# A fused attention pair: the weight stream in twelve slices through four places, and another order of the first loads

## The chip, the cores and the metric

The kernel runs on one core of one Trainium2 chip. What counts is the device time of one execution in microseconds (us). Before the change three runs took 1550.25, 1554.49 and 1554.56 us, so the median is 1554.49 us.

## What is computed

Two attentions read the same x (1 x 2048 x 640, bf16) and are mixed by a gate.

```python
g = sigmoid((x * gate_w).sum(-1, keepdims=True))
a = A(x)          # 64 segments in turn, each needs the memory of the one before
b = B(x)          # local, dilated
out = g * a + (1 - g) * b

# A: H = 32 heads of 192, segment of 32 tokens, 8 memory rows
for s in range(64):
    h = concat([mem, x[32*s : 32*s+32]])             # 40 rows of 640
    q, k, v = h @ Wq, h @ Wk, h @ Wv                 # each W is 640 x 6144
    p = softmax(mask(q @ k.T * 192**-0.5))           # per head
    o = (p @ v) @ Wo                                 # Wo is 6144 x 640
    mem = o[:8];  outs.append(o[8:])

# B: 32 heads of 20; each position looks at 8 positions, 2 apart, backwards
q, k, v = split(x @ wqkv);  b = (softmax(q . k[pos - 2*j]) @ v) @ wo
```

A's weights are four matrices of 640 x 6144 bf16, 31 MB in all. They don't all fit into the core's on-chip memory beside the working tiles, and each of the 64 segments needs all of them.

## The kernel before

**Stages.** Part B comes first (0 to about 187 us). Behind it a prepass (to about 345 us) works out what of A's q, k and v doesn't depend on the running memory. Then part A runs: segment 0 on its own, 62 segments in a loop (380 to 1461 us), the last segment, and `part_z`, which makes the rows of the output that the memory rows stood for.

**Slices of A's weights.** A's weights are cut into slices: `("q", p, kc)` and `("k", p, kc)` with 15 of each, `("v", t, kc)` with 15, `("oa", i)` with 12 and `("ob", i)` with 8. A slice of q, k or v has 128 rows of 2048 bf16 numbers (4096 bytes a row, 512 KB), one of oa or ob 128 rows of 1536 (384 KB). A fourth or third index in the key (`_is_half`) makes it a half slice: 256 KB or 192 KB. `_parts` says whether a slice is used whole or as two halves.

**Resident and streamed.** Most slices stay in the core for all of part A. `weights_setup` (L511) orders them and deals them out: the first `N_EARLY` are loaded in part B, the next `N_EARLY2` and then `late` follow as memory of other stages becomes free, and the last `N_LAST` in segment 0 (`load_late(2)`, L1045). The tiles of the late ones are named `wlate_...`. What is in the list `STREAM` is loaded again in every segment, through `SLOTS` places (tiles `wst0`, `wst1`, ...), in the order in which TensorE uses it. `pump` (L558) issues the next load on SP's queue whenever the place that it falls to is free; the place of load n is n modulo `SLOTS`. `release` (L566) marks a place free when TensorE has issued the last matmul that reads its slice, and calls `pump`. The load itself waits on SP, at L562, until those matmuls have ended. So each place is in one of three states: in use, being filled, or waiting filled. Before the change 21 half slices go through seven places of 2 KB a partition.

**Order.** In part A, and in part B from `order.enter_context` on (L400), the order of instructions on each engine is the one written. Ahead of that point, for the short block's projection `proj(0, n, c)` (L379 to L381), the order comes from a scheduler. The loop's segments are cut into stages (`stage`, L788): at each boundary every engine, SP too, waits for what the stage before left open (L1133 is the line that these waits carry). In the loop no loads are issued between `held()` and the next `stage()`.

**Part B's beginning.** Part B works in blocks of 484 positions and one short block ahead of them (block 0). `proj(b, n, c)` (L263) makes 128 rows of q or k of a block and stores them to DRAM on SP's queue (L276); `load_qk` (L278) reads them back with the heads laid out afresh, as `bqT` and `bkT`, four loads for each; `scores` (L296) needs these. `load_xT(b, ...)` (L190) loads 512 tokens of x. `make_v` (L252) makes v; `gates` (L225) the gate. `bulk` (L390) is a list of loads that are issued a few at a time by `fetch`: x, B's output weights, the early resident slices, and for the prepass the columns of Wq.

**The prepass** reads Wq and Wk by columns (`get_columns`, L588), from resident slices where there are any, and otherwise by loads into the places of the stream, which aren't used for streaming yet: on SP's queue for q, on POOL's for k. The slices of v that aren't resident are loaded there on POOL's queue (`get_slice`).

Of the kernel before, what the change touches and what calls it, by code (L numbers as in the profile page):

```python
# [10 lines left out]
BF = mybir.dt.bfloat16  # L11
F32 = mybir.dt.float32
I32 = mybir.dt.int32

SLOTS = 7
N_EARLY = 15
N_EARLY2 = 12
N_LAST = 7
LATE0 = 71680
STREAM = [("q", 0, 1, 1), ("k", 0, 1, 1), ("k", 0, 3, 1), ("q", 1, 1, 0), ("k", 1, 0, 0), ("k", 1, 3, 1), ("q", 2, 2,  # L20
          0), ("k", 2, 0, 1), ("k", 2, 1, 1), ("k", 2, 4, 1), ("v", 0, 3, 1), ("v", 1, 1, 0), ("v", 1, 4, 1), ("v", 2,
          0, 1), ("v", 2, 3, 0), ("oa", 3, 1), ("oa", 4, 1), ("ob", 2, 0), ("oa", 7, 0), ("oa", 11, 0), ("ob", 6, 0)]

STEP_PE = 3.4

# [7 lines left out]
def _width(key):  # L33
    n = 1536 if key[0] in ("oa", "ob") else 2048
    return n // 2 if _is_half(key) else n

def _parts(key):
    halves = [key + (h,) for h in range(2)]
    return halves if any(k in STREAM for k in halves) else [key]

# [53 lines left out]
class _K:  # L94
# [59 lines left out]
    def part_b(self, outer):  # L154
# [11 lines left out]
        with ExitStack() as ctx:  # L166
# [23 lines left out]
            def load_xT(b, q, t0=0, t1=512):  # L190
                return q.dma_start(xT[:, :, HALO + 512 * b + t0:HALO + 512 * b + t1], self.laid["xT"][:, :, 512 * b + t0:512 * b + t1])
# [5 lines left out]
            load_xT(0, nc.sync)  # L197
            nc.scalar.dma_start(gw[:], self.laid["gw"].unsqueeze(2))
            nc.scalar.dma_start(wv[:], self.laid["wv"])
            load_xT(1, nc.sync)  # L200
            ones = wp.tile([128, 32], BF, name="b_ones")
            nc.vector.memset(ones[:], 1.0)
            band = wp.tile([128, NQ], BF, name="band")
# [71 lines left out]
                self.evac(t[:, 0:nn], ps[:, 0:nn], "dve" if n == 0 or b > 1 else "act")  # L275
                nc.sync.dma_start(qk_dram[b, n][128 * c:128 * c + 128], t[:, 0:nn])  # L276

            def load_qk(b, queue=None):  # L278
                for n in range(2):
                    nn = shape_of(b)[0] * shape_of(b)[1] + n * HALO  # L280
                    for hh in range(4):
                        (queue or nc.sync).dma_start(QK[n][b % 2][32 * hh:32 * hh + 20, :, 0:nn], heads(qk_dram[b, n], 0, 8, hh))
# [93 lines left out]
            nc.scalar.preload_act_table_set("natural_log_exp_and_others")  # L376
            assert S % 512 == 0 and nb == 5
            steps = [(b, g) for b in range(nb) for g in range(8)]
            for c in range(KC):  # L379
                for n in range(2):  # L380
                    proj(0, n, c)  # L381
# [12 lines left out]
            def fetch(n):  # L394
                for f, *a in bulk[:n]:
                    f(*a)
                del bulk[:n]

            order = ExitStack()
            order.enter_context(tc.manual_schedule(engines={mybir.EngineType.PE, mybir.EngineType.Activation, mybir.EngineType.DVE,  # L400
                                                            mybir.EngineType.SP, mybir.EngineType.Pool}))
            fetch(1)
            make_v(0, range(2))
            proj(1, 0, 0)
            proj(1, 1, 0)
            load_qk(0, nc.scalar)
            gates(0)

            def fill(what):
                for w in what:  # L410
# [24 lines left out]
            rest = tasks  # L435
# [57 lines left out]
    def v_columns(self, t, kc):  # L493

        out = []
        for k in _parts(("v", t, kc)):
            sl = self.get_slice(k)
            out += [sl[:, f:f + 512] for f in range(0, _width(k), 512)]
        return out
# [11 lines left out]
    def weights_setup(self):  # L511
        nc, tc = self.nc, self.tc
        rest = [k for u in _slice_keys() for k in _parts(u) if k not in STREAM]
        first = ["q", "k", "v", "oa", "ob"]
        rest = sorted(rest, key=lambda k: first.index(k[0]))
        self.early, self.early2, late = rest[:N_EARLY], rest[N_EARLY:N_EARLY + N_EARLY2], rest[N_EARLY + N_EARLY2:]
        self.late = ([], [], late[-N_LAST:])
        used = 0
        for k in late[:-N_LAST]:
            used += 2 * _width(k)  # L520
            self.late[int(used > LATE0)].append(k)
        self.wres = self.ctx.enter_context(tc.tile_pool(name="wres", bufs=1))
        self.res_tiles = {}
        at = _places()[0]
        self.packed = {k: self.laid["slices"][n:n + 128 * _width(k)].rearrange("(p f) -> p f", p=128) for k, n in at.items()}
        self.wscr = self.packed
        self.wstream = self.ctx.enter_context(tc.tile_pool(name="wstream", bufs=1))
        self.slots = [self.wstream.tile([128, 1024], BF, name=f"wst{i}") for i in range(SLOTS)]
        self.slot_at, self.streaming, self.pending = 0, False, []

    def load(self, key, t):
# [42 lines left out]
    def get_slice(self, key):  # L574
        if key in self.res_tiles:
            return self.res_tiles[key]
        n = _width(key)
        if self.streaming:
            assert STREAM[self.used] == key and self.used < self.sent
            t = self.slots[self.used % SLOTS][:, 0:n]  # L580
            self.used += 1
            return self.view(t, key)
        t = self.slots[self.slot_at % SLOTS][:, 0:n]
        self.slot_at += 1
        self.nc.gpsimd.dma_start(t, self.wscr[key])
        return self.view(t, key)

    def get_columns(self, m, h):  # L588

        W = {"q": self.Wq, "k": self.Wk}[m].rearrange("(c p) f -> p c f", p=128)  # L590
        p, x = h // 2, h % 2
        out = {}
        for kc in range(self.KC):
            if (m, p, kc) in self.res_tiles:
                t = self.res_tiles[m, p, kc][:, 1024 * x:1024 * x + 1024]
            else:
                t = self.slots[self.slot_at % SLOTS]
                self.slot_at += 1
                (self.nc.sync if m == "q" else self.nc.gpsimd).dma_start(t[:], W[:, kc, 1024 * h:1024 * h + 1024])
            out[kc] = [t[:, f:f + 128] for f in range(0, 1024, 128)]  # L600
        return out

# [97 lines left out]
    def part_a(self):  # L700
# [4 lines left out]
        with ctx:  # L705
# [28 lines left out]
                        return x[:, f:f + 32]  # L734

            st = [Px[2], Px[1], KW[:, 512:1024], Px[2]]
            st4 = self.slots[1][:, 768:1024], Px[0][:, 0:256]
            st5 = (P[1][:, 1:5, 0:8, :].rearrange("p b c i -> p b (c i)"), Px[0][:, 256:512])

            psm = ctx.enter_context(tc.tile_pool(name="psm", bufs=1, space=bass.MemoryType.PSUM))  # L740
# [44 lines left out]
            def segment(part, prev, s, nxt, looped=False):  # L785
# [278 lines left out]
                if nxt is None:  # L1064
                    self.oz, self.oz_keys = {}, {}
                    self.oz_free = [k for p in range(3) for m in "qk" for k in self.res_tiles if k[:2] == (m, p) and len(k) == 3]
                    self.oz_free += [k for k in self.res_tiles if k[0] == "v" and len(k) == 3]
                    self.b4_free = [k for k in self.res_tiles if k[0] in "vqk" and len(k) == 4]
                    self.load_oz(0)
                if nxt is not None:  # L1070
                    load_seg(nxt)
# [97 lines left out]
    def part_z(self, psm, wo, tail):  # L1169

        nc = self.nc
        oz = self.oz
        kept = self.kept.values()
        for i, k in enumerate(k for k in STREAM if k in wo and k not in kept):
            t = self.res_tiles[self.b4_free[4 + i]][:, 0:_width(k)]
            nc.sync.dma_start(t, self.wscr[k])
            wo[k] = self.view(t, k)
        for n in range(1, 4):
            if n > 1:
                self.load_oz(n)  # L1180
            self.sort_oz(n)
        for n in range(4):
            b4 = self.res_tiles[self.b4_free[n]][:, 0:640]
            rows = lambda ap: ap.rearrange("(n s t) f -> n s t f", n=4, t=32)[n, :, 24:32, :]
            nc.scalar.dma_start(b4.bitcast(I32).rearrange("p (j f) -> p j f", j=4),
                                self.bsc_dram.rearrange("(n s t) j f -> n s t j f", n=4, t=32)[n, :, 24:32, :, 0:80])
            for part, f0, nf in (("oa", 0, 384), ("ob", 384, 256)):
                ps = psm[int(part == "ob")]
                for c in range(48):
                    R, j, t = c // 12, c // 3 % 4, c % 3  # L1190
                    for q in range(4):
                        nc.tensor.matmul(ps[32 * q:32 * q + 32, 0:nf],  # L1192
                                         lhsT=oz[n, q][:, 24 * (1 - R // 2) + 6 * j + 3 * (R % 2) + t, :],
                                         rhs=self.o_weights(wo, part, c), start=(c == 0), stop=(c == 47),
                                         tile_position=(0, 32 * q), skip_group_check=True)
                nc.vector.scalar_tensor_tensor(out=b4[:, f0:f0 + nf], in0=ps[:, 0:nf], scalar=self.gZ[:, n:n + 1],  # L1196
                                               in1=b4[:, f0:f0 + nf], op0=ALU.mult, op1=ALU.add)
            nc.sync.dma_start(rows(self.out2d), b4)
            if n == 0:
                tail()  # L1200
# [63 lines left out]
```

## Time and profile before

| what | value |
|---|---|
| median of the runs | 1554.49 us |
| the profiled execution | 1550.84 us |
| its span (first to last instruction) | 1548.8 us |
| part B, prepass | 0 to about 187, to about 345 us |
| segment 0 | 345.6 to about 376 us |
| the loop, 62 iterations | 379.7 to 1461.2 us, 17.445 us each |
| last segment and `part_z` | to 1548.8 us |
| TensorE busy (matmul, by the profile's model) | 1459.2 us, 94% |
| bytes moved | 446.3 MB, mean 288 GB/s |

PE is TensorE, PEld its weight loads, DVE VectorE, ACT ScalarE, POOL GpSimd, SP the engine that only issues DMAs; "SPq" is SP's queue. A row such as `L916 PE MATMUL psm<-wst,aHa` is the matmuls of line 916 that read a place of the stream (`wst`) and a working tile (`aHa`) and write into the tile `psm`. The clock in the profile is the TensorE clock that was granted, where 1.00 is full speed. The DMA share is the mean busy share of the core's 16 DMA engines. In the list of DMA issues, the last number is the median time from issue to landing. All times are of one profiled execution.

### The profile page before, as it was taken

How to read it: one execution, taken by the hardware profiler on the slowest of the kernel's cores; microseconds unless marked ns; L12 is line 12 of the kernel's file. 1: busy time of each engine (PE TensorE's matmuls, PEld its weight loads, DVE VectorE, ACT ScalarE, POOL GpSimd, SP SyncE). 2: the span in 40 equal slices, each digit the busy share in tenths (PEclk: the TensorE clock that was granted, in tenths of full speed). 3: DMA queues.
4: the chain of work that ended last, by engine and by line, in shares of the span. 5: the costliest groups of instructions: out<-in, count | busy, mean ns of one | idle time of the engine just before them, and what ended most of it. 6: DMA issues, size and time to landing. Idle time of an engine off the chain costs nothing. (4 is left out here: it accounts for less than half of the span.)

```text
span 1548.8 us, 91126 instructions
## 1 busy us (share of the span) xinstructions
PE 1459.2 (94%) x36746; PEld 821.3 (53%) x36746; DVE 815.6 (53%) x2256; ACT 642.7 (41%) x1673; POOL 205.9 (13%) x432
## 2 busy tenths in 40 slices
PE   5988899997999999999999999999999999999978
PEld 3444444443555555555555555555555555555557
DVE  1787533333555555555555555555555555555510
ACT  1587532222443444344443444444444444344430
POOL 0000200200111111111111111111111111111100
PEclk9999999998999999999999999999999999999989
DMA  6778896788999999999999999999999999999970
GB/s 174 199 194 229 275 310 167 178 264 284 303 318 321 333 322 316 316 329 322 325 323 330 327 326 317 321 337 324 327 322 326 324 324 321 328 322 329 314 192 16
DMA packets 365435, 446.30 MB, mean 288 GB/s; under 512 B 123864, under 2 KB 227848, under 8 KB 365368
## 3 DMA queue, kind: packets, MB, share of 16 engines
q1 hardware_dynamic: 271080, 395.47, 77.7%
q10 hardware_dynamic: 80736, 25.44, 6.9%
q0 software_dynamic: 13552, 24.47, 4.9%
q8 instruction: 46, 0.75, 0.2%
q14 instruction: 21, 0.17, 0.0%
HBM read 407.04 MB, written 38.20 MB: 287 GB/s over the span
## 5 line engine op out<-in xcount | busy, mean ns | idle before, releaser
L825 ACT CAST aP<-psx 128x512 bf16<-128x512 f32 x128 | 68.7, 589 | 358.2 <-PE psx L818 358.2
L980 PEld LDWEIGHTS <-aP 128*32 128x32 bf16 x6144 | 162.7, 96 | 63.9 <-ACT aP L959 20.3
L916 PE MATMUL psm<-wlate_v,aHa 128*32 128x512 bf16 x2048 | 189.6, 381 | 1.1 <-issue 1.1
L818 PEld LDWEIGHTS <-aHa 128*32 128x32 bf16 x4608 | 120.1, 96 | 119.1 <-issue 20.6
L980 PE MATMUL psm<-wlate_oa,aP 128*32 128x384 bf16 x2560 | 167.7, 329 | 0.0
L840 DVE STREAM_TRANSPOSE aK<-aP 128x512 bf16<-128x512 bf16 (+1 forms) x256 | 135.0, 546 | 7.6 <-ACT aP L825 0.8
L980 PE MATMUL psm<-wst,aP 128*32 128x384 bf16 (+1 forms) x896 | 121.4, 306 | 7.4 <-DMA wst<-in_slices_dram 7.4
L980 PE MATMUL psm<-wlate_ob,aP 128*32 128x256 bf16 x2688 | 125.8, 274 | 1.0 <-issue 1.0
L818 PE MATMUL psm<-wres_q,aHa 128*32 128x512 bf16 x1280 | 119.2, 382 | 7.4 <-PEq L1133 5.2
L959 DVE CAST aP<-psx 128x128 bf16<-128x128 f32 (+2 forms) x192 | 75.6, 422 | 80.2 <-PE psx L947 80.1
L837 DVE STREAM_TRANSPOSE aP<-aP 128x512 bf16<-128x512 bf16 (+1 forms) x128 | 74.1, 579 | 79.1 <-ACT aP L825 79.1
L916 PE MATMUL psm<-wlate_v,aHb 128*32 128x512 bf16 x1152 | 115.2, 379 | 0.0
L818 PEld LDWEIGHTS <-aHb 128*32 128x32 bf16 x3072 | 77.3, 96 | 60.5 <-issue 3.0
L818 PE MATMUL psx<-wres_k,aHa 128*32 128x512 bf16 x896 | 108.1, 381 | 0.0
L925 ACT CAST aP<-psm 128x256 bf16<-128x256 f32 (+1 forms) x192 | 85.9, 447 | 47.7 <-PE psS L870 46.3
L959 ACT CAST aP<-psS 128x384 bf16<-128x384 f32 (+2 forms) x192 | 65.3, 374 | 72.5 <-PE psx L947 48.3
L756 POOL DMA_DIRECT2D aVz<-zv_dram x64 | 34.3, 535 | 443.2 <-DMA wst<-in_slices_dram 397.1
L818 PE MATMUL psx<-wst,aHa 128*32 128x512 bf16 x512 | 88.5, 382 | 2.1 <-DMA wst<-in_slices_dram 2.1
L818 PE MATMUL psm<-wres_q,aHb 128*32 128x512 bf16 x1024 | 80.4, 381 | 0.0
L916 PEld LDWEIGHTS <-aHa 128*32 128x32 bf16 x2304 | 54.7, 97 | 46.4 <-issue 16.4
L749 POOL DMA_DIRECT2D aK<-in_xh_dram x63 | 34.4, 546 | 329.0 <-PE psm L916 289.1
L941 PEld LDWEIGHTS <-aP 32*128 32x128 bf16 (+1 forms) x4096 | 43.4, 97 | 64.5 <-DVE aK L907 32.8
(181 smaller groups left out, 3222.3 us busy)
## 6 DMA issues: line engine op xcount, KB each, us to landing
wst<-in_slices_dram SPq DMA_DIRECT2D x960, 256.0 KB, 4.7
wst<-in_slices_dram SPq DMA_DIRECT2D x384, 192.0 KB, 3.8
zpk_dram<-ZS ACTq DMA_DIRECT2D x6, 2048.0 KB
aP<-zpk_dram SPq DMA_DIRECT2D x64, 192.0 KB, 3.9
wres_q<-in_slices_dram SPq DMA_DIRECT2D x12, 512.0 KB
aVz<-zv_dram POOLq DMA_DIRECT2D x64, 96.0 KB, 4.4
wlate_v<-in_slices_dram SPq DMA_DIRECT2D x10, 512.0 KB
wst<-in_A_Wk_dram POOLq DMA_DIRECT2D x14, 256.0 KB, 5.9
```

The source lines that it names most:

```text
L749: nc.gpsimd.dma_start(xh, row(self.xh_dram, s))
L756: nc.gpsimd.dma_start(vz[:], self.zv_dram[bass.ds(8 * s, 8)].rearrange("i r f -> r i f"))
L818: burst([nc.tensor.matmul(pq[32 * j:32 * j + 32, :], lhsT=hT[kc], rhs=sl[j], start=(kc == 0), stop=(kc == KC - 1), tile_position=(0, 32 * ...
L825: nc.scalar.copy(st[i], pqs[i])
L837: nc.vector.transpose(P[p][:, 1:5, c0:c1, :].rearrange("p b c i -> p c b i"), x)
L840: nc.vector.transpose(KT[:, c0:c1, :].rearrange("p c k -> p (c k)"), x)
L916: burst([nc.tensor.matmul(pvs[t][32 * j:32 * j + 32, :], lhsT=hT[kc], rhs=sl[j], start=(kc == 0), stop=(kc == KC - 1), tile_position=(0, 3 ...
L925: (nc.vector.tensor_copy if t == 0 else nc.scalar.copy)(Px[t][:, cs], pvs[t][:, cs])
L941: ms.append(nc.tensor.matmul(out[:, r, t, :], lhsT=v_block(2 * h + r, t)[ks, f0 - 128 * t:f1 - 128 * t], rhs=E[ks, par, EA.start + 40 * r: ...
L959: (nc.scalar.copy, nc.vector.tensor_copy)[g](x.rearrange("p (j c q) -> p j c q", j=2, q=32), pairs[g][:, :, 0:240].rearrange("p j (c q) -> ...
L980: ms.append(nc.tensor.matmul(pso[part][32 * jj:32 * jj + 32, 0:n], lhsT=oT_slot(R // 2, j, 3 * (R % 2) + t), rhs=self.o_weights(osl, part, ...
```

## The change

**The stream.** `STREAM` names twelve slices in place of 21 halves: six whole slices of q, k and v (512 KB), three half slices (256 KB) and three whole slices of oa and ob (384 KB). They go through four places: the first of 2 KB a partition, the other three of 4 KB. A place is used by every fourth load, so the three half slices, loads 1, 5 and 9, all fall to the small place.

**The prepass.** The four places count as seven pieces of 2 KB there (`pieces`). `get_piece` hands them out in turn. A slice of v that is streamed whole is loaded in two pieces. With other slices resident, the columns of Wq take four loads and no longer six, and those of Wk eight and no longer 14; three of these eight, and no longer one, stand at the head of POOL's queue.

**Resident slices.** `N_EARLY`, `N_EARLY2` and `N_LAST` go from 15, 12, 7 to 14, 9, 6, with the same bytes in each of the three sets; half slices are sorted behind the whole ones of a kind.

**Part A.** In segment 0 six and no longer seven late loads are issued; oa(0) is issued ahead of them and oa(3), ob(4) and the next q(0,0,1) behind. The staging place of one part of k (`st4`) moves to another quarter of place 1. The tail takes the four tiles for its mix from the list `oz_free`.

**Part B's beginning.** The written order now starts ahead of `proj(0)`. On SP's queue `load_xT(1)` comes behind the ten stores of `proj(0)`. The four loads of `bqT` follow `make_v` on ScalarE's queue, and the four of `bkT` follow `load_xT(1)` on SP's. `proj(1)` comes behind both, and `fetch(1)`, which issues x's third block, behind `gates(0)`.

```diff
-SLOTS = 7
-N_EARLY = 15
-N_EARLY2 = 12
-N_LAST = 7
+SLOTS = 4
+N_EARLY = 14
+N_EARLY2 = 9
+N_LAST = 6
-STREAM = [("q", 0, 1, 1), ("k", 0, 1, 1), ("k", 0, 3, 1), ("q", 1, 1, 0), ("k", 1, 0, 0), ("k", 1, 3, 1), ("q", 2, 2,
-          0), ("k", 2, 0, 1), ("k", 2, 1, 1), ("k", 2, 4, 1), ("v", 0, 3, 1), ("v", 1, 1, 0), ("v", 1, 4, 1), ("v", 2,
-          0, 1), ("v", 2, 3, 0), ("oa", 3, 1), ("oa", 4, 1), ("ob", 2, 0), ("oa", 7, 0), ("oa", 11, 0), ("ob", 6, 0)]
+STREAM = [("q", 0, 0, 1), ("k", 0, 1), ("k", 0, 2), ("k", 1, 0), ("k", 1, 2, 0), ("q", 2, 3), ("v", 0, 0), ("v", 1, 2),
+          ("v", 2, 0, 0), ("oa", 0), ("oa", 3), ("ob", 4)]
...
             nc.scalar.dma_start(wv[:], self.laid["wv"])
-            load_xT(1, nc.sync)
...
-            def load_qk(b, queue=None):
-                for n in range(2):
+            def load_qk(b, queue=None, ns=range(2)):
+                for n in ns:
...
+            order = ExitStack()
+            order.enter_context(tc.manual_schedule(...))
             for c in range(KC):
                 for n in range(2):
                     proj(0, n, c)
...
-            order = ExitStack()
-            order.enter_context(tc.manual_schedule(...))
-            fetch(1)
+            load_xT(1, nc.sync)
             make_v(0, range(2))
+            load_qk(0, nc.scalar, (0,))
+            load_qk(0, nc.sync, (1,))
             proj(1, 0, 0)
             proj(1, 1, 0)
-            load_qk(0, nc.scalar)
             gates(0)
+            fetch(1)
...
         for k in _parts(("v", t, kc)):
+            if k in STREAM and not self.streaming and not _is_half(k):
+                for f in (0, 1024):
+                    sl = self.get_piece(self.wscr[k][:, f:f + 1024], self.nc.gpsimd)
+                    out += [sl[:, 0:512], sl[:, 512:1024]]
+                continue
...
-        rest = sorted(rest, key=lambda k: first.index(k[0]))
+        rest = sorted(rest, key=lambda k: (first.index(k[0]), _is_half(k)))
...
-        self.slots = [self.wstream.tile([128, 1024], BF, name=f"wst{i}") for i in range(SLOTS)]
+        self.slots = [self.wstream.tile([128, 2048 if i else 1024], BF, name=f"wst{i}") for i in range(SLOTS)]
+        self.pieces = [t[:, x:x + 1024] for i, t in enumerate(self.slots) for x in range(0, 2048 if i else 1024, 1024)]
...
+    def get_piece(self, src, queue):
+        t = self.pieces[self.slot_at % len(self.pieces)]
         self.slot_at += 1
-        self.nc.gpsimd.dma_start(t, self.wscr[key])
-        return self.view(t, key)
+        queue.dma_start(t, src)
+        return t
...
-            st4 = self.slots[1][:, 768:1024], Px[0][:, 0:256]
+            st4 = self.slots[1][:, 1536:1792], Px[0][:, 0:256]
...
-                    self.b4_free = [k for k in self.res_tiles if k[0] in "vqk" and len(k) == 4]
+                    self.b4_free = [self.oz_free.pop() for _ in range(4)]
...
-        for i, k in enumerate(k for k in STREAM if k in wo and k not in kept):
-            t = self.res_tiles[self.b4_free[4 + i]][:, 0:_width(k)]
-            nc.sync.dma_start(t, self.wscr[k])
-            wo[k] = self.view(t, k)
+        assert all(k in kept for k in STREAM if k in wo)
```

## The prediction

> **What bounds the kernel now.** I read the page's totals and slices first, then the windows by stage, then the waits of TensorE and of SP, then the DMA issues. The first three lines below are busy time per engine, the granted clock and the DMA engines' share in 40 slices of 38.7 us.
>
> ```profile
> span 1548.8 us, 91126 instructions
> PE 1459.2 (94%) x36746; PEld 821.3 (53%) x36746; DVE 815.6 (53%) x2256; ACT 642.7 (41%) x1673; POOL 205.9 (13%) x432
> PEclk9999999998999999999999999999999999999989
> DMA  6778896788999999999999999999999999999970
> q1 hardware_dynamic: 271080, 395.47, 77.7%
> wst<-in_slices_dram SPq DMA_DIRECT2D x960, 256.0 KB, 4.7
> wst<-in_slices_dram SPq DMA_DIRECT2D x384, 192.0 KB, 3.8
> ```
>
> TensorE is busy for 94% and the DMA engines are nearly full from slice 9 on: two resources are close to the bound at once. The last two lines are the stream: 960 + 384 = 1344 loads, 21 in each of 64 segments, and each takes about 4 us from issue to landing. The windows (columns: length, PE, PEld, DVE, ACT, POOL busy, clock, DMA share, GB/s) split this by stage:
>
> ```profile
> 20.00:28.00 8.00, 2.27 (x28) 1.15 (x26) 0.61 (x3) 0.75 (x2) 0.00 (x0) 0.93 0.64 152
> 28.00:34.00 6.00, 5.81 (x21) 2.46 (x22) 1.81 (x5) 1.28 (x3) 0.00 (x0) 0.52 0.16 49
> 191.00:192.00 1.00, 1.00 (x6) 0.45 (x5) 0.00 (x0) 0.00 (x0) 0.00 (x0) 1.00 1.07 418
> 361.00:367.00 6.00, 0.97 (x28) 0.69 (x24) 1.00 (x4) 0.68 (x3) 0.93 (x2) 0.82 1.03 377
> 367.00:372.00 5.00, 5.00 (x92) 3.16 (x87) 1.30 (x5) 0.00 (x0) 0.00 (x0) 0.53 0.98 339
> 376.00:380.00 4.00, 0.52 (x8) 0.17 (x8) 1.68 (x3) 0.59 (x1) 0.00 (x0) 0.81 0.69 225
> 400.00:800.00 400.00, 390.28 (x11649) 223.71 (x11648) 227.37 (x688) 170.57 (x503) 62.20 (x115) 1.00 0.96 321
> 1503.00:1545.00 42.00, 41.68 (x1152) 33.05 (x1143) 3.28 (x7) 0.00 (x0) 0.00 (x0) 0.94 0.11 28
> ```
>
> The loop (380 to 1461 us, 62 iterations) is 70% of the span: TensorE 97.6% busy at full clock, DMA share 0.96. Around it stand three holes, each followed by a spell at half clock: 20 to 28, 361 to 367, 376 to 380. The waits of TensorE, from the first 40 us and then from 400 to 1400 us, say on what (total us, times, longest):
>
> ```profile
> PE ps_bS L296 <- DMA bkT<-bk_dram: 5.6, 1, 5.6
> PE ps_bqk L271 <- DMA xT<-in_xT_dram: 4.7, 1, 4.7
> ...
> PE psm L916 <- DMA wst<-in_slices_dram: 4.9, 15, 0.7
> PE psx L818 <- DMA wst<-in_slices_dram: 0.9, 3, 0.4
> ```
>
> **The loop's stream.** One iteration takes 1081.6 / 62 = 17.445 us, and the mean of the eight fastest is 17.00. By the start times of matmuls, v(2,0,1) (L916) costs TensorE a mean 0.30 us an iteration and k(0,1,1) 0.09. The listed waits carry less, 5.8 us in 1000, because a late matmul's neighbours hide part of it. So a stream that is never late is worth between 5.8 x 1.08 = 6 and 62 x 0.39 = 24 us.
>
> Removed are 9 of 21 loads an iteration; the bytes stay (15 x 256 + 6 x 192 KB = 3 x 256 + 6 x 512 + 3 x 384 KB = 4992 KB). The trace's DMA packets in the loop last 94 ns at 2048 B a row, 75 at 1536, 132 at 3072; rows of 4096 B (the loads of resident slices near 190 us) last 173. A load has 128 rows, eight on each of 16 DMA engines, so a segment costs each engine 15 x 8 x 94 + 6 x 8 x 75 ns = 14.9 us before and (3 x 94 + 6 x 173 + 3 x 132) x 8 ns = 13.7 us after: 1.15 us or 7.7% less, against a loop that has the engines at 0.96. SP issues nine loads fewer at 0.33 to 0.45 us each; it is not on the path, but it waits L1133 for landings at each of four stage boundaries (58.4 us in 1000), with fewer semaphores to clear after.
>
> Against this stands grain. The places hold 14 KB a partition as before, but there are four. A place can be refilled only when its slice is released, and must have landed by its next use. From the matmuls' start times those spaces were 4.7 to 6.4 us before. In the new order they are 6.1, 5.2, 4.9, 4.3, 3.9, 4.1 us for q(0,0,1), k(0,1), k(0,2), k(1,0), k(1,2,0), q(2,3), and 4.9 to 6.6 for the six behind. The quickest 256 KB loads of the loop land on average 3.2 us after issue; a 512 KB load adds 8 x (173 - 94) ns = 0.6, so 3.8 with nothing ahead of it. k(1,2,0) and q(2,3) then have 0.7 and 0.3 us to spare, and k(0,2), issued right behind k(0,1), about 0.4. Before, loads with a mean spare time of 0.36 and 0.14 us cost 0.09 and 0.30 us an iteration.
>
> By halfway, where v(2,0,1) is late, the engines have saved about 0.6 us, so its 0.30 goes; the three edge loads, like those rows, give back some 0.2 of the 0.39. I take 62 x (0.39 - 0.22) = 10 us gained. Ends: 24 gained; and lost 62 x 1.05 = 65, if k(1,2,0) and q(2,3) need the 4.9 and 5.1 us that the fifth and sixth loads took from issue to landing before. I stay far from that end because those loads waited in a queue of up to seven that the four places cannot build.
>
> **The front.** Before, SP issued xT(1) behind xT(0) at once; its bytes ran ahead of the stores of the short block (proj(0)), which TensorE needs back as bqT and bkT. All eight of those loads went out on ScalarE's queue, 20.8 to 27.4 us, and scores began at 28.04, after 5.6 us of idle. After, xT(1) follows the ten stores, the four bqT loads go on ScalarE's queue and the four bkT loads on SP's behind xT(1); proj(1) and xT(2) come later. Queued on SP behind the last bkT load, which waits for xT(1) to land (eight completions a queue are in use in turn), are proj(1)'s stores, xT(2) and the bulk loads, none of which TensorE needs before 34 us. Added to POOL at the start are two more Wk column loads (three for one, 512 KB, at the 320 GB/s of the loop 1.6 us of a busy start). I estimate stores out at 16 to 17, xT(1) landed at 20.5 to 22.5 where it was 18.3, proj(1) in the old hole, scores at 24.8 to 26.4: 2.4 us earlier. The hole before proj(1) is then 3.3 to 3.7 us. The half clock of 26.9 to 33.8 (5.81 us busy at 0.52, so 2.8 us lost) followed a hole of 5.6 us; the shorter one I count as sparing 1.6 of the 2.8. Gain 4 us; ends 6.5, and a loss of 1.5 if xT(1) lands at the late end and the spell returns. Part B behind it (34 to 187, TensorE 134 of 153 us) should pass the gain on; DMA share there is 0.80.
>
> The Trainium skill (TensorE: Matmul & The Clock Gate, Part 1: The HAM clock gate) has the clock halved after a whole idle window of about 3.4 us, and the window runs free. The trace agrees in length: half-clock spells are 3.4, 6.8 or 10.3 us long. By that rule a hole of 3.5 us seldom holds a whole window, and the front would bring 5.2 us.
>
> **Segment 0 and the loop's entry.** ob(2,0) lands 5.0 us late at 361.6 because SP issued seven late resident loads (`wlate`) ahead of it, and the spell to 371.7 costs half of the 5.00 us busy, 2.5. After, six such loads (2304 KB, as before) stand between oa(0) and oa(3); oa(3) meets them, and as its place was freed earlier I estimate 2.3 us of wait and no spell: 2.7 + 2.5 gained. The loop's entry (3.5 us, L1133) waits for landings that the same bytes push back, say 1 to 2 us more. Net 3 gained; ends 7 gained, 1.5 lost.
>
> **What costs nothing.** The prepass loads 2 MB less (Wq 6 to 4 and Wk 14 to 8 columns); TensorE is busy 155 of 158 us there, so nothing is gained, and the cover would be gone only if a column came late, which fewer loads make less likely. Resident sets hold the same bytes (6912, 4608, 2304 KB) in fewer loads. TensorE's matmuls are the same. The new place of a staged k (`st4`) lies where the next stream load in that place, oa(0), does not reach, so it adds no wait. The tail takes its tiles for the mix from the other end of one list; its 42 us of matmuls are untouched: 0, ends 1 either way.
>
> **Sum.** The profiled execution took 1550.84 us (span 1548.8 and 2.0 around it), 3.65 under the median of the runs, whose lowest is 1550.25. 1550.8 - 4 - 3 - 10 = 1533.8; the runs scatter by about 4 upward, and I add half: 1536.
>
> **Rivals.**
> - Grain decides: k(1,2,0), q(2,3) and k(0,2) are late by 0.5 us more an iteration. For it: spaces of 3.9 and 4.1 us against landings of 4.9 and 5.1. Against: the shorter queue and 7.7% less DMA work. 1550.8 - 7 + 31 + 2 = 1577; it is slower than before from 0.11 us an iteration on.
> - The stream is never late: 1533.8 - 14 + 2 = 1522. For it: 1.15 us saved against 0.39 lost. Against: spare times as small as those that cost time before.
> - Long rows bring nothing: bytes, not packets, bind. For it: 321 to 326 GB/s all through the loop. Against: 418 GB/s at 191 us with rows of 4096 B. Only front and segment 0 gain: 1550.8 - 7 + 2 = 1546. The Trainium skill (DMA: Bandwidth & Descriptors, Where 436 GB/s comes from) puts a core's HBM share at about 358 GB/s, which speaks for this; the 418 measured here stands above it.
>
> **Chances.** Likeliest 0.50 (own range 1526 to 1547), grain 0.24, never late 0.14, bytes 0.12. Range for 8 in 10: 1520 to 1567, so that the better part of the grain case and little else lies outside. About 0.3% (4.7 us) is what a measurement of this kernel tells from no change; under 1549.8 lie nearly all of three cases, 0.66; within it the edges of the likeliest and of bytes and the mildest grain, 0.12; slower 0.22.
>
> **What would show it.** Right: iterations of 17.2 to 17.35 us, no wait at the v(2,0) slice, packets of 173 ns, DMA share near 0.89 with 321 GB/s or more; scores before 26.5 us with no half clock behind; a wait on oa(3) of 2 to 3 us in segment 0 in place of 5.0 on ob(2,0). Wrong: waits of TensorE on `wst` at L818 for k(0,2), k(1,2,0) or q(2,3) above 0.3 us an iteration, which is the forecast's weakest step; or xT(1) landing after 23 us, which turns the front's gain into a loss.

## The result and the profile after

The changed kernel is slower: 1648.61 us (median of four runs, 1637.27 to 1661.92) against 1553.28 us for the kernel before (four runs), a ratio of 1.061 (1.057 to 1.064). The run of 1661.92 us is a slow one, and the ratio is that of the others. The forecast was 1536 us, between 1520 and 1567. Its rival on the slower side, "grain decides", had the right sign and a quarter of the size.

The profiled execution took 1637.27 us. First the page's totals of the changed kernel, its clock and DMA share in 40 slices, and the stream's loads:

```profile
span 1635.3 us, 89257 instructions
PE 1477.9 (90%) x36746; PEld 820.5 (50%) x36746; DVE 815.6 (50%) x2254; ACT 641.6 (39%) x1673; POOL 203.5 (12%) x426
PEclk9999999989999999999999999999999999999989
DMA  7888886887999899989989998889989999889880
q1 hardware_dynamic: 187232, 395.07, 73.8%
wst<-in_slices_dram SPq DMA_DIRECT2D x384, 512.0 KB, 5.6
wst<-in_slices_dram SPq DMA_DIRECT2D x192, 384.0 KB, 4.2
wst<-in_slices_dram SPq DMA_DIRECT2D x192, 256.0 KB, 3.6
```

The bytes on SP's queue are the same (395 MB) and the DMA share has fallen: the engines stand idle more. The loads moved the same weight in fewer pieces, and the 512 KB ones take 5.6 us from issue to landing. Then the windows of the changed kernel by stage (length, busy time of PE, PEld, DVE, ACT, POOL, clock, DMA share, GB/s):

```profile
18.00:22.00 4.00, 0.74 (x6) 0.38 (x5) 0.48 (x1) 0.42 (x1) 0.00 (x0) 0.85 0.73 202
22.00:28.00 6.00, 5.85 (x34) 2.51 (x35) 1.18 (x4) 0.69 (x2) 0.00 (x0) 0.53 0.29 67
358.00:363.00 5.00, 0.63 (x27) 0.27 (x25) 0.24 (x2) 0.40 (x2) 0.54 (x1) 0.57 1.05 390
800.00:1200.00 400.00, 366.15 (x10867) 206.22 (x10854) 212.07 (x640) 159.75 (x473) 58.49 (x108) 1.00 0.90 299
```

In 400 us of the loop TensorE now works 366 us and no longer 390 to 392, at full clock, and the DMA share is 0.90 where it was 0.96 to 0.97. What TensorE waits for, from 400 to 1400 us (total us, times, longest):

```profile
PE psx L826 <- DMA wst<-in_slices_dram: 46.8, 63, 1.3
PE psm L924 <- DMA wst<-in_slices_dram: 11.3, 30, 1.0
PE psS L878 <- issue: 5.6, 24, 0.6
PE psm L826 <- DMA wst<-in_slices_dram: 3.7, 6, 1.4
```

L826 is the line of the q and k matmuls (L818 before), L924 that of v. The listed waits on `wst` were 5.8 us in the same stretch before and are now 61.8.

By stage, from the times of matmuls in the two profiled executions (us; the loop from its first matmul to the end of its last):

| stretch | before | after | difference |
|---|---|---|---|
| start to the prepass | 186.4 | 183.7 | -2.7 |
| prepass | 157.1 | 155.6 | -1.5 |
| segment 0 up to the loop's entry | 36.1 | 35.8 | -0.3 |
| the loop | 1081.6 | 1174.4 | +92.8 |
| behind the loop | 87.6 | 85.8 | -1.8 |

Everything outside the loop got 6 us better and the loop got 92.8 worse: 18.9 us an iteration for 17.4.

**Where in the iteration.** For each load of the stream I took, over the iterations, the mean time at which its place came free, at which it was issued and landed, and at which TensorE first used it, with the first matmul of `tail` as zero. "Start to start" is the time from the start of the matmul ahead of that first use to its own; it grows when TensorE has to wait. The two loads that matter, beside the rows of the kernel before that answer to them:

| load | place free | issued | landed | used | start to start of the matmuls there |
|---|---|---|---|---|---|
| before: k(0,1,1) | -5.41 | -5.21 | -0.89 | -0.53 | 0.09 |
| before: k(0,3,1) | -4.46 | -4.40 | 0.35 | 0.88 | 0.03 |
| after: k(0,1) | -6.87 | -6.83 | -1.84 | -1.48 | 0.21 |
| after: k(0,2) | -6.39 | -6.35 | -0.37 | -0.33 | 1.14 |

k(0,2) is used as it lands, in every iteration, and its wait of about 1.1 us is the larger part of the 1.5 that an iteration lost. The other new wait is v(1,2): 0.56 from start to start. SP is not the cause: it issues within 0.3 us of the place coming free for all loads but ob(4), 0.6, and within 0.04 for these two.

### The profile page after: what moved, and what is told of

Read it like the earlier page. It is cut to its first block, busy times and chain, and to the rows that moved or that the text cites. A ratio compares the mean times of both kernels' runs of the same rounds, so it can differ in the third digit from the quotient of the medians.

```text
span 1635.3 us, 89257 instructions
## 1 busy us (share of the span) xinstructions
PE 1477.9 (90%) x36746; PEld 820.5 (50%) x36746; DVE 815.6 (50%) x2254; ACT 641.6 (39%) x1673; POOL 203.5 (12%) x426
## 5 line engine op out<-in xcount | busy, mean ns | idle before, releaser
L826 PEld LDWEIGHTS <-aHa 128*32 128x32 bf16 x4608 | 121.7, 96 | 188.4 <-issue 91.1
L988 PEld LDWEIGHTS <-aP 128*32 128x32 bf16 x6144 | 166.8, 96 | 53.8 <-ACT aP L967 13.8
L924 PE MATMUL psm<-wlate_v,aHa 128*32 128x512 bf16 x1664 | 148.7, 380 | 1.0 <-issue 1.0
L988 PE MATMUL psm<-wlate_oa,aP 128*32 128x384 bf16 x2560 | 147.2, 329 | 0.0
L826 PE MATMUL psx<-wst,aHa 128*32 128x512 bf16 x640 | 75.6, 387 | 56.0 <-DMA wst<-in_slices_dram 55.9
L826 PE MATMUL psm<-wres_q,aHa 128*32 128x512 bf16 x1536 | 117.6, 383 | 4.1 <-PEq L1141 4.0
L933 ACT CAST aP<-psm 128x256 bf16<-128x256 f32 (+1 forms) x192 | 85.9, 447 | 87.6 <-PE psS L878 86.5
L924 PE MATMUL psm<-wlate_v,aHb 128*32 128x512 bf16 x1536 | 117.6, 379 | 0.0
L826 PEld LDWEIGHTS <-aHb 128*32 128x32 bf16 x3072 | 70.8, 97 | 73.2 <-DVE aK L848 7.6
L887 DVE TENSOR_TENSOR aK<-aK,aSel 128x224 bf16<-128x224 bf16 x128 | 35.2, 275 | 120.5 <-ACT aK L886 120.5
L924 PE MATMUL psm<-wst,aHa 128*32 128x512 bf16 x640 | 75.4, 383 | 14.2 <-DMA wst<-in_slices_dram 13.7
L924 PEld LDWEIGHTS <-aHa 128*32 128x32 bf16 x2304 | 56.4, 96 | 58.8 <-issue 29.2
L878 PEld LDWEIGHTS <-aK 128*32 128x32 bf16 (+1 forms) x4096 | 45.8, 91 | 67.5 <-issue 34.1
L826 PE MATMUL psx<-wres_k,aHa 128*32 128x512 bf16 x1024 | 78.7, 383 | 0.0
```

Of the source, the lines that this page charges most:

```text
L826: burst([nc.tensor.matmul(pq[32 * j:32 * j + 32, :], lhsT=hT[kc], rhs=sl[j], start=(kc == 0), stop=(kc == KC - 1), tile_position=(0, 32 * ...
L878: ms.append(nc.tensor.matmul(out, lhsT=k, rhs=q, start=(half == 0 and R2 == 0), stop=(half == 1 and R2 == 2), tile_position=(ks.start, 32 ...
L887: nc.vector.tensor_tensor(out=E, in0=E, in1=self.mask[h].unsqueeze(1).to_broadcast([128, 2, 112]), op=ALU.mult)
L924: burst([nc.tensor.matmul(pvs[t][32 * j:32 * j + 32, :], lhsT=hT[kc], rhs=sl[j], start=(kc == 0), stop=(kc == KC - 1), tile_position=(0, 3 ...
L933: (nc.vector.tensor_copy if t == 0 else nc.scalar.copy)(Px[t][:, cs], pvs[t][:, cs])
L988: ms.append(nc.tensor.matmul(pso[part][32 * jj:32 * jj + 32, 0:n], lhsT=oT_slot(R // 2, j, 3 * (R % 2) + t), rhs=self.o_weights(osl, part, ...
```

## The experiments

Three theories for the loss in the loop. **P**, positions: what counts is how evenly the uses of streamed slices lie over the iteration; k(0,1) and k(0,2) are neighbours in TensorE's order and 0.22 us apart when nothing waits, so 1 MB falls due at once. **G**, grain: a place of 4 KB comes free only when a whole slice has been read, so less is under way. **L**, length: a 512 KB load with rows of 4096 bytes is itself slow. All ratios are to the kernel before on the same chip, with 95% intervals; iterations are means from each run's trace without the loop's first (17.40 in the kernel before). The front alone, the stream alone, the halves and the two DMAs ran on one chip, all the others in this table on another.

| kernel | us (median) | ratio | iteration |
|---|---|---|---|
| after, repeated | 1644.70 | 1.059 (1.051 to 1.066) | 19.1 |
| front alone | 1551.83 | 1.002 (0.999 to 1.004) | 17.42 |
| stream alone | 1673.96 | 1.077 (1.072 to 1.083) | 19.7 |
| after's slices, 21 halves, seven places | 1620.25 | 1.044 (1.040 to 1.049) | 18.64 |
| after, two DMAs for a slice | 1636.55 | 1.056 (1.052 to 1.061) | 18.87 |
| after, two slices exchanged | 1611.94 | 1.041 (1.036 to 1.047) | 18.44 |
| after, one slice exchanged | 1620.38 | 1.044 (1.041 to 1.047) | 18.66 |
| before, room in lumps of two | 1575.11 | 1.016 (1.011 to 1.022) | 17.84 |
| before, one bunch of four halves | 1639.01 | 1.059 (1.052 to 1.066) | 18.91 |
| before, two halves exchanged | 1543.14 | 0.996 (0.994 to 0.998) | 17.31 |
| the same with the front | 1547.82 | 0.998 (0.996 to 1.000) | 17.38 |

### The front alone

The kernel before, with the new order of part B's beginning and nothing else:

```diff
-            load_xT(1, nc.sync)
...
-            fetch(1)
+            load_xT(1, nc.sync)
             make_v(0, range(2))
+            load_qk(0, nc.scalar, (0,))
+            load_qk(0, nc.sync, (1,))
             proj(1, 0, 0)
             proj(1, 1, 0)
-            load_qk(0, nc.scalar)
             gates(0)
+            fetch(1)
```

> The kernel before with only the new order of part B's beginning. By the trace of after, the first q and k projections of part B end 3.9 us sooner and the prepass starts 2.7 us sooner, although TensorE still runs at half clock for 6 us there. So I expect the loop to be reached 2.5 to 4 us sooner than before and the time to fall by as much, a ratio of 0.997 to 0.999, with iterations unchanged at 17.4 us. If the front only moves a wait into part B or the prepass, the ratio is 1.000.

Measured: 1.0015 (0.9991 to 1.0040). In its trace the prepass starts 2.2 us sooner and the loop 2.3 us sooner, but the runs do not show it at the end: the loop took 1085.5 us in that trace, for 1081.6 before. The hole before proj(1) is 5.6 us there (16.99 to 22.60) where the changed kernel had 3.3; scores start at 28.9 us, not sooner than before (28.04).

### The stream alone

The changed kernel with the old front (the diff above, reversed).

> The changed kernel with the old order of part B's beginning: the twelve slices through four places alone. If the whole loss is in the loop and the front is a gain by itself, this is 2 to 4 us slower than the changed kernel, with iterations of 18.9 us. If the front had anything to do with the loop's loss, the iterations would be shorter.

Measured: 1.077, slower than the changed kernel by more than the intervals leave room for. The sign was right and the size was not: I expected 2 to 4 us and found about 25. This run and the repeat of the changed kernel were on different chips, so a part of the 25 may come from there. The iterations of 19.7 us are those of the profiled execution, at 1689 us the longest of the four. The places of the waits in it are those of the changed kernel, k(0,1) 0.68 and k(0,2) 1.26 us from start to start, only longer: k(0,1) lands 5.65 us after its issue, and 5.00 in the changed kernel. A part of it is the clock, 0.98 in its loop:

```profile
800.00:1200.00 400.00, 358.50 (x10440) 200.82 (x10432) 203.79 (x616) 153.26 (x453) 55.92 (x103) 0.98 0.87 286
```

The clock was halved for 3.4 us twelve times in this loop, twice in the changed kernel's and five times in that of its repeat. One such spell costs half of its 3.4 us at most, so the ten more explain at most 17 of the 50 us by which the two profiled loops differ. Why the loads land later, and whether an order that lies 300 us ahead of the loop has to do with it, I can't say. With the even stream of the kernel before, the front moves no iteration (17.42 for 17.40). This stays open.

### The same slices as halves, through seven places

```diff
-SLOTS = 4
+SLOTS = 7
-STREAM = [("q", 0, 0, 1), ("k", 0, 1), ("k", 0, 2), ("k", 1, 0), ("k", 1, 2, 0), ("q", 2, 3), ...
+STREAM = [("q", 0, 0, 1), ("k", 0, 1, 0), ("k", 0, 1, 1), ("k", 0, 2, 0), ("k", 0, 2, 1), ("k", 1, 0, 0), ...
...
-[128, 2048 if i else 1024]
+[128, 1024]
```

(`st4` lies in place 1 as before the change, and a slice that is streamed as both halves is read in the order of its halves.)

> The changed kernel, the same twelve slices streamed, but as 21 half slices through seven places of 2 KB. Theory G (grain: a 4 KB place comes free only when its whole slice has been read, so less can be under way and the DMA engines stand idle): iterations of 17.3 to 17.6 us, 1545 to 1555 us. Theory P (the choice of slices: two whole k slices used 1.1 us apart, behind a stretch of output weights that are resident): iterations stay above 18.4 us, 1610 us or more. Theory L (a 512 KB load with rows of 4096 bytes is itself slow) gives what G gives here.

Measured: 1620.25 us, 18.64 us an iteration. That is P's answer, with some G in it: with the places, sizes and count of loads of the kernel before, and only the choice of slices and the front of the changed one, most of the loss is still there. The intervals of this run (1.040 to 1.049) and of the changed kernel (1.051 to 1.066) don't meet, so the finer places give back about 24 us, the two being measured on different chips, each against the kernel before. Its waits from 400 to 1400 us:

```profile
PE psx L827 <- DMA wst<-in_slices_dram: 33.6, 100, 0.8
PE psS L879 <- issue: 6.6, 21, 0.8
PE psm L925 <- DMA wst<-in_slices_dram: 0.4, 1, 0.4
```

The waits on v (L925) have gone, with the fine places; those on k (L827) stay, in smaller steps: both halves of k(0,2) come up at 0.7 us, one behind the other.

### Two DMAs for a whole slice

```diff
-            self.nc.sync.dma_start(self.slots[n][:, 0:_width(k)], self.wscr[k])
+            h = _width(k) if _is_half(k) else _width(k) // 2
+            for f in range(0, _width(k), h):
+                self.nc.sync.dma_start(self.slots[n][:, f:f + h], self.wscr[k][:, f:f + h])
```

> The changed kernel, four places as they are, but each whole slice brought by two DMAs, one for each half of the place, so 21 loads and rows of 2048 and 1536 bytes. Theory L: iterations fall back to 17.3 to 17.6 us. Theory G, and P: the place still comes free as a whole, so 18.6 to 19.0 us and 1620 to 1650 us; what there is of a gain is that the first half can be used before the second has landed, at most some 0.3 us an iteration.

Measured: 1.056 (1.052 to 1.061), within the interval of the changed kernel's repeat. Rows of 2048 and 1536 bytes and loads of 256 and 192 KB in the same four places don't help: L falls. The wait at k(0,2) is 1.4 us from start to start. v(1,2), which can now be used half by half, drops from 0.56 to 0.26.

### The changed kernel once more, and two slices exchanged

The first is the changed kernel as it is, run beside the two slices exchanged, the room in lumps and the one bunch.

> The changed kernel itself, as the measure for the three others on this chip: iterations of 18.9 us, a ratio of 1.057 to 1.064.

Measured: 1644.70 us, 1.059, iterations of 19.1 us. The second spreads the uses and leaves places and sizes alone; q(2,4) for q(2,3) goes with the two:

```diff
-STREAM = [..., ("k", 0, 1), ("k", 0, 2), ..., ("q", 2, 3), ..., ("oa", 0), ("oa", 3), ("ob", 4)]
+STREAM = [..., ("k", 0, 1), ("k", 0, 3), ..., ("q", 2, 4), ..., ("oa", 0), ("oa", 5), ("ob", 4)]
```

> The changed kernel with two of the twelve slices exchanged for others that are used later: k(0,3) for k(0,2), and oa(5) for oa(3) (and q(2,4) for q(2,3), which is used one step later, so that a slice of the same group stays). Places, sizes and bytes stay. In the old order k(0,1) and k(0,2) are used 0.2 us apart and oa(0) and oa(3) 0.5 apart; now 1.4 and 1.6 us. Theory P (slices that are used close behind one another, 1 MB due within a fraction of a microsecond): iterations fall by 0.4 to 0.9 us, to 18.0 to 18.5, 1590 to 1625 us. Theory G (the size of the places): iterations within 0.15 us of the changed kernel's.

Measured: 1611.94 us, 18.44 us an iteration: 33 us of the 95 come back from three names in a list. The trace's waits from 400 to 1400 us:

```profile
PE psm L924 <- DMA wst<-in_slices_dram: 16.9, 32, 1.1
PE psm L826 <- DMA wst<-in_slices_dram: 9.1, 25, 1.2
PE psS L878 <- issue: 7.9, 35, 0.3
PE psx L826 <- DMA wst<-in_slices_dram: 1.3, 5, 0.3
```

The 46.8 us on `psx` at L826, where k(0,1) and k(0,2) are read, have become 1.3; the waits have moved on to k(1,0), with k(1,2,0) close behind it (`psm` at L826), and to v(1,2).

### One slice exchanged

Only k(0,3) for k(0,2); oa(3) and q(2,3) stay.

> The changed kernel with one slice exchanged alone, k(0,3) for k(0,2), so that two whole k slices are used 1.4 us apart and no longer 0.2; oa(0) and oa(3) stay 0.5 us apart. If the pair of k slices carries what the exchange of two slices brought (34 us, iterations of 18.44 us), this is 18.4 to 18.6 us an iteration and 1605 to 1625 us; if the pair of oa slices does, it stays at 18.8 us or more, 1635 us or more.

Measured: 1620.38 us, 18.66 us. By time the k pair carries 24 of the 33 us; the iteration is 0.06 us above the range that I gave it. The remaining 8 us belong to the oa pair and q(2,4) together. What the two slices exchanged left of the loss, 62 us, was not taken apart: the waits on k(1,0) and v(1,2) stand in that trace, and the next experiment gives a price for grain.

### Before, with room in lumps

The even stream and the seven places of the kernel before, but `pump` issues an even-numbered load only when the place behind it is free too:

```diff
+        def free():
+            i, p = self.sent % len(STREAM), self.sent % SLOTS
+            pair = i % 2 == 0 and i + 1 < len(STREAM) and self.sent >= SLOTS
+            return not self.busy[p] and not (pair and self.busy[(p + 1) % SLOTS])
-        while (...) and not self.busy[self.sent % SLOTS]:
+        while (...) and free():
```

> The kernel before, with its 21 evenly spread half slices and seven places, but a load is issued only when the places of two neighbouring loads are both free, so that room comes free in lumps of 512 KB as with four places. Theory G: iterations rise by 0.5 us or more, to 17.9 or above, 1580 us or more. Theory P: they stay within 0.25 us of 17.4, 1550 to 1565 us.

Measured: 1.016 (1.011 to 1.022), 25 us more, 17.84 us an iteration. It lies between the two forecasts. So grain costs by itself, 0.44 us an iteration, and about as much as the third experiment gave back (24 us).

```profile
PE psm L921 <- DMA wst<-in_slices_dram: 19.4, 31, 1.2
PE psS L946 <- ACT aP L930: 2.7, 16, 0.2
PE psm L823 <- PE psm L823: 0.8, 3, 0.4
PE psx L823 <- DMA wst<-in_slices_dram: 0.7, 2, 0.4
```

The wait is on v (L921): v(1,4,1) is issued 1.1 us after its place is free, since it waits for the place of v(2,0,1), and then comes 0.65 us late.

### Before, with one bunch

The kernel before, 21 halves through seven places, with the k halves of its first two groups moved together (and `N_EARLY2` at 10, which keeps the bytes of each resident set; a slice streamed as both halves is read in the order of its halves):

```diff
-STREAM = [("q", 0, 1, 1), ("k", 0, 1, 1), ("k", 0, 3, 1), ("q", 1, 1, 0), ("k", 1, 0, 0), ("k", 1, 3, 1), ...
+STREAM = [("q", 0, 1, 1), ("k", 0, 1, 0), ("k", 0, 1, 1), ("k", 0, 2, 0), ("k", 0, 2, 1), ("q", 1, 1, 0), ...
```

> The kernel before, 21 half slices through seven places, with three of them exchanged so that k(0,1) and k(0,2) are streamed whole, four halves used within 0.4 us, in place of halves of k(0,1), k(0,3), k(1,0) and k(1,3), used over 3.3 us. Places, load sizes, bytes and number of loads stay. Theory P: iterations rise by 0.6 us or more, to 18.0 or above, 1590 us or more, with waits of TensorE on the streamed slices at the k(0,2) matmuls. Theory G: 17.4 to 17.6 us, 1550 to 1565 us.

Measured: 1639.01 us, 1.059 (1.052 to 1.066), 18.91 us an iteration. With small places, small loads and the same bytes, one bunch costs as much as the whole change. The waits of TensorE from 400 to 1400 us:

```profile
PE psx L818 <- DMA wst<-in_slices_dram: 53.9, 139, 1.1
```

and a window of its loop, with the columns as above:

```profile
800.00:1200.00 400.00, 372.43 (x10823) 208.71 (x10818) 210.95 (x638) 158.52 (x469) 57.32 (x106) 1.00 0.91 298
```

There is one line of waits, and it is the k matmuls: 0.67, 0.78 and 0.70 us from start to start at k(0,1,1), k(0,2,0) and k(0,2,1). A 256 KB load occupies the DMA engines for 8 x 96 ns = 0.77 us (its packets' mean in this trace), so TensorE takes the four halves at the pace of the engines. The places that these four loads need come free one after another over 2.0 us, from -7.2 to -5.2, at the even pace of the slices used there, while their uses lie within 0.4 us when nothing waits. And the DMA share is 0.91 where it was 0.97: the engines can't work ahead for the bunch, since no place is free to take it. This settles P: a bunch by itself is enough for such a loss.

### A more even stream

Two halves of the kernel before exchanged, the other way round from the bunch:

```diff
-          0, 1), ("v", 2, 3, 0), ... ("ob", 6, 0)]
+          1, 1), ("v", 2, 3, 0), ... ("ob", 5, 0)]
```

(v(2,1,1) for v(2,0,1) and ob(5,0) for ob(6,0).)

> The kernel before with two of its 21 half slices exchanged: v(2,1,1) for v(2,0,1), used 0.2 us later in an empty stretch of 1.6 us, and ob(5,0) for ob(6,0), used 0.6 us earlier, so that the place behind it comes free earlier. Theory P (what counts is how evenly the uses lie): the wait of 0.3 us at the v(2,0) slice falls by about half, 17.25 to 17.35 us an iteration, 4 to 10 us less than before, a ratio of 0.994 to 0.998. If the waits before had another cause, the ratio is 1.000 within 0.002.

Measured: 0.996 (0.994 to 0.998), 1543.14 us, 17.31 us an iteration. The matmuls of the v(2) slice stand 0.15 us from start to start where the kernel before had 0.32 in the same reckoning. This version beats both kernels, the one before by 0.4%.

> The same with the new order of part B's beginning. The front alone measured a ratio of 1.0015 (0.9991 to 1.004), so I expect this within 0.003 of the run without it; if the front's 2 to 4 us sooner are carried to the end, it is 0.001 to 0.003 lower.

Measured: 0.998 (0.996 to 1.000). The front adds nothing here either.

## Why the prediction was wrong, point by point

**"the three edge loads, like those rows, give back some 0.2 of the 0.39" and the sum's 10 us gained.** This is the step that failed. It put three loads at 0.2 us an iteration, and k(0,2) alone cost 1.1. I compared each load's space with what a load takes "with nothing ahead of it", and gave k(0,2), "issued right behind k(0,1), about 0.4" to spare. The two have to be taken together. From the issue of k(0,1) to the landing of k(0,2) the trace shows 6.46 us. Its parts: 1.5 us from issue to the first packet, while q(0,0,1) is still being moved; 4.4 us of packets, of which 2 x 8 x 191 ns = 3.1 are those of the two loads and 24 x 28 ns = 0.7 those of the 192 KB of `aP`, issued just ahead, and 0.6 I did not break up further (POOL's and ScalarE's transfers lie in it); 0.5 to the landing. From oa(0)'s release to the use of k(0,2) there are 5.2 + 0.2 = 5.4 us when nothing waits. The difference, 1.1 us, is the wait that was measured. Most of these terms, not the length of the long packets, could be had from the trace of before. The forecast had named a wait for k(0,2) among the signs of being wrong.

The spare times were too large for a second reason. The 3.2 us that I took for the quickest 256 KB loads are those of ob(2,0), which has 192 KB; the quickest of 256 KB in that trace, q(0,1,1), lands 3.8 us after its issue. With 3.8, and so 4.4 for 512 KB, k(1,2,0) has 0.1 us to spare and q(2,3) and k(0,2) have none, even one by one.

**The bad end of that step.** "lost 62 x 1.05 = 65" was no bound: the loop lost 92.8. I had drawn it from landings in a steady queue, where places come free one at a time.

**"1.15 us or 7.7% less" work for the DMA engines.** It did not come. In the loop rows of 4096 bytes last 191 ns, not 173, and rows of 3072 bytes 152, not 132; those of 2048 take 88. Neither 173 nor 132 came from the loop of the kernel before: 173 is for rows near 190 us, and 132 for those on SP's queue in segment 0. A segment costs (3 x 88 + 6 x 191 + 3 x 152) x 8 ns = 14.9 us, as before. The rival "long rows bring nothing" was right in this, and wrong in its time, since it left the rest of the loop as it was. Per iteration the engines work 0.97 x 17.4 = 16.9 us before and 0.90 x 18.9 = 17.0 after. Work is the same; idle time grew from 0.5 to 1.9 us.

**The rival "grain decides".** Right in sign; its price of 0.5 us an iteration is near what grain alone costs (0.44). Its places were wrong: k(1,2,0) and q(2,3), with the smallest spaces, are hardly late (0.21 and 0.31 us from start to start, against 0.21 in undisturbed matmuls around them), since TensorE's wait at k(0,2) just ahead gives them time. The mechanism that decided, the bunch, was in none of the rivals.

**"I stay far from that end because those loads waited in a queue of up to seven."** It fails with the first point: the queue was not what made landings long. With at most four places outstanding the 512 KB loads took 5.6 us.

**The front, 4 us.** The prepass did start 2.7 us sooner, but not for the reason that I gave. The hole before proj(1) is 3.3 us (18.65 to 21.91), as estimated, and xT(1) landed within the estimate. Yet the clock fell to half all the same (0.53 from 22 to 28 us, above), so the "1.6 of the 2.8" was not spared, and scores began at 28.3 us and not at 24.8 to 26.4. What is left of the gain is that proj(1) is done ahead of the scores. Alone, the front measured no change. Nor does the new order always give 3.3 us: in the other seven traces with the new front the hole lasted 3.1 to 5.6 us, and half clock followed all but one, of 3.95 us (two DMAs for a slice). The rule of the Trainium skill (TensorE: Matmul & The Clock Gate, Part 1: The HAM clock gate), one whole idle window of about 3.4 us, from which I had drawn that a hole of 3.5 us would seldom halve the clock, did not hold up here: 3.3 us sufficed.

**Segment 0, 3 us.** 0.3 measured. The mechanism was right and its size was not. The late slice is oa(3), as forecast: it is issued at 353.1 us behind the six late loads and lands at 362.4. But TensorE waits 4.4 us for it and not 2.3, and the half clock, which I had taken to be gone, comes with it (0.57 in the window from 358 us). The waits of TensorE there, from the prepass's end to the loop in the changed kernel:

```profile
PE psm L988 <- DMA wst<-in_slices_dram: 4.4, 1, 4.4
PE psm L826 <- PEq L1141: 2.3, 1, 2.3
PE psx L826 <- DVE ZV L142: 2.1, 1, 2.1
PE psS L955 <- issue: 1.4, 1, 1.4
```

The loop's entry waits 2.3 us where it waited 3.5 and where I had added 1 to 2.

**What was to cost nothing.** The prepass gained 1.5 us: a wait of 1.4 us on a column at 282 us in the trace of before is gone. Behind the loop 1.8 us were gained, where I had given 1 either way; which part did it was not tried.

**The sum.** Outside the loop I forecast 7 us gained and the profiled executions show 6, but not by the terms forecast: the front and segment 0 gave 3 of their 7, and the rest came from stages put at nothing. In the loop I forecast 10 gained and 92.8 were lost.

## What to carry to other kernels

When a ring of buffers feeds an engine and the DMA engines are nearly full, a list of what is streamed is a schedule: lay the uses out in time, with the bytes due at each, and compare every stretch with what the engines move in it. Two neighbours are costed as one load, from the release of the first one's buffer to the use of the second, with everything that is queued among them; a table of spaces one by one hides this. Fewer, larger loads cost their grain here and, with rows of 2 KB to start with, brought nothing back.

## What was not expected of the hardware

A row of 4096 bytes took 173 ns in the prepass and 191 in the loop, against 88 to 98 for one of 2048 bytes in all the kernels here: at these sizes an engine moves 20 to 24 bytes per ns whatever the row's length. A hole of 3.3 us was followed by half clock. Shorter ones were too: in the loop of the changed kernel the clock was halved at 696.6 and 1451.0 us, and in the 3.4 us ahead of each TensorE had been busy 1.5 us, with no hole longer than 1.1 us. And the changed kernel's loop took 18.9 to 19.1 us an iteration with the new front and 19.7 in the one profiled execution with the old one, while the even stream's stayed at 17.4; no run here shows why.
